# Attention with plain products on 64x32 and 64x64 tiles of the array, in front of an unchanged two-layer network

## The chip, the cores and the metric

The kernel runs on one core of a Trainium2 chip. The metric is the device time of one launch in microseconds (us). The core has a matrix engine (TensorE, called PE in the profile, with its weight loads as PEld), a vector engine (VectorE, DVE), an activation engine (ScalarE, ACT), a general engine (GpSimd, POOL), and queues that start DMA transfers (SP above all). Products are summed in PSUM, which has 8 banks of 128 partitions x 512 fp32 words; everything else lives in SBUF or in DRAM.

## The reference

Inputs are q, k, v of 8 batches x 8 heads x 576 positions x 64, and the network's weights (512 x 2048, 2048 x 512) and slopes.

```
scores = scale * np.matmul(q, k.transpose(0, 1, 3, 2))        # scale = 1/8
mask = block_i >= block_j                                      # blocks of 64 positions
scores = np.where(mask, scores, -1000000000.0)
scores = scores - np.max(scores, axis=-1, keepdims=True)
attn = np.exp(scores)
attn = attn / (np.sum(attn, axis=-1, keepdims=True) + 1e-09)
x = np.matmul(attn, v)            # then heads side by side: 4608 tokens x 512
h = x @ w_in
g = np.maximum(h, 0.0) + alpha * np.minimum(h, 0.0)
out = g @ w_out
```

A query block T (of nine, 0 to 8) sees the T + 1 key blocks 0 to T.

## The kernel before

**Two stages.** The 64 (batch, head) problems are taken as 32 pairs of heads, p = 0 to 31, four pairs to a batch. In the first stage attention of all pairs runs, and between its steps the network is computed for the first 6 of 16 feature groups (FA = 6) on chunks of 256 tokens (`chunk_a`: `ffn1` at L586, `activate` at L597 to L606, `ffn2` at L623, partial sums to DRAM). When attention has ended and the rest of these chunks too, the second stage takes the other 10 groups with chunks of 512 tokens (`factors`, `pair1` at L664, `ffn2` again) by a scheme of seven products in place of eight. There every operand is split into a high and a low part (hi, lo), each of which TensorE multiplies in one pass (type fp32r), and three products stand for one fp32 product.

**Attention per pair.** `prep` loads q, k and v, splits q and k into hi and lo (L745, L747, L750, L751), and lays them out by ten DMAs on the SP queue as stacked operands Q and K of 128 rows, in which hi and lo parts and the rows of a mask share one product. `query_tile` takes a tile j of 128 queries with all keys that any of them sees: products (L848, for the last 64 queries of both heads L921), a row maximum on DVE (L866, L872, L927), exp with row sums on ACT (L875, L934), the reciprocals on DVE, a scaling on POOL (L883, L941), transposes of 128x128 blocks on PE by a product with the identity (L891, L947, L956), and copies out of PSUM as hi (L970, ACT) and lo (L971, DVE). `values` multiplies with v: three products for one, again (L1004), and an ACT copy and a DVE sum that move the two parts together (L1023, L1025). For the first pairs (p below 5 in `values`, fewer in `query_tile`) plain fp32 products are used instead, which PE takes in two passes each: L853 (two heads on the two halves of the array's rows, 64x128 each), L856 (the mask), L915, L994 and L998.

**Weights.** `to_f32` (L468 to L485) makes fp32 words out of the 64-bit floats that are loaded, with five DVE instructions and one ACT instruction per 128x512 weights, and two PSUM banks for what lies between. `split` (L491, L492) makes hi on ACT and lo on POOL or DVE.

**Order.** Every instruction is handed to a planner (`Plan.op`, with an engine, a cost, the tiles it reads and writes and a priority), and `Plan.schedule` writes the order of every engine's queue and of every buffer's uses once, before the launch. `LAG` says by how many pairs the chunks run behind attention, `SHIFTS` changes single priorities, `BANKS`, `HB` and `AB` share the PSUM banks out: 6 for attention and weights, 1 for `ffn1`, 1 for `ffn2`.

Of the kernel before, what the change touches and what calls it, by code (L numbers as in the profile page):

```python
# [9 lines left out]
F32 = mybir.dt.float32  # L10
# [10 lines left out]
NP = H // 2  # L21
# [9 lines left out]
NEG = -1.0e30  # L31
SM = 512
QP = S + 64
PW = 1920
# [4 lines left out]
C0, C1 = 3.0, 4.0  # L39
WARM, WARM_END = 10, 3400  # L40
TICK, FULL_COLUMNS, SP0 = 3413.33, 3060, 700
LAG = 6.75
Q2B, TB = 1, 1
VP, VL, VE = 2.0, 1.0, 0.0
E0, E1 = -4.0, 1.0
NEAR, LP = 8.0, 1.0
FP = -1
XP = 2.0
AHEAD = {(8 + k // 2, k % 2): 12 + 4 * k for k in range(4)}
SHIFTS = {  # L50
# [6 lines left out]
}  # L57
SOON, XB = 150, 1006.7
FEW = 12
# [4 lines left out]
NV = NP + 1  # L64
PB = 6
# [8 lines left out]
IN_ORDER = {"qraw", "kraw", "vraw", "QH", "QL", "KH", "KL", "Q", "K", "V", "raw", "m", "xb", "X", "xt"}  # L74
# [16 lines left out]
class Plan:  # L91
# [44 lines left out]
    def schedule(self):  # L136
# [43 lines left out]
        while events:  # L180
# [13 lines left out]
            for engine, heap in ready.items():  # L194
# [12 lines left out]
                if engine == "PE" and before:  # L207

                    c, light = self.ops[chosen][1], None
                    if before.short and not c.light:  # L210
                        light = True
                    elif not before.short and c.light and not c.short:
                        light = False
                    if light is not None:
                        others = sorted(x for x in heap if (self.ops[x[1]][1].light if light else self.ops[x[1]][1].short)
                                        and x[0] < self.ops[chosen][5] + NEAR)
                        other = next((x for x in others if lacks(x[1]) is None), None)
                        if other:
                            heap.remove(other)
                            heap.append((self.ops[chosen][5], chosen))  # L220
                            heapq.heapify(heap)
                            chosen = other[1]
# [8 lines left out]
                if engine == "PE":  # L231
                    saved = before.short if before and cost.light else 0.0
# [52 lines left out]
HALF = 126  # L285
# [6 lines left out]
class Products:  # L292


    def __init__(self, full, rest, columns, short=0.0, light=False):
        self.full, self.rest, self.columns = full, rest, columns
        self.short, self.light = short, light

    def __add__(self, o):
        return Products(self.full + o.full, self.rest + o.rest, self.columns + o.columns) if o else self  # L300

    __radd__ = __add__
# [7 lines left out]
def c_mm(n, rows=P):  # L310
    return Products(max(n / 2.22, 107) + 2, max(n / 1.2, 213), n * rows / P)


def c_tr(light=False):
    return Products(109, 213, 256, 50.0, light)


def c_one(n, light=False):

    c = c_mm(n)  # L320
    return Products(c.full, c.rest, c.columns, c.full - max(n / 2.22 + 2, 57), light)
# [3 lines left out]
def attn_ffn(ctx, tc, qT, kT, vT, w_in, w_out, alpha, out):  # L325
# [14 lines left out]
    ident = const.tile([P, P], F32, name="ident")  # L340
    make_identity(nc, ident)
    mask_l = const.tile([P, P], BF16, name="mask_l")
    mask_r = const.tile([P, 64], BF16, name="mask_r")
    nc.vector.memset(mask_l, 0.0)
    nc.vector.memset(mask_r, 0.0)
    for i in range(2):
        nc.vector.memset(mask_l[64 * i:64 * i + 1, 0:64], 1.0)
        nc.vector.memset(mask_r[64 * i:64 * i + 1, :], NEG)
    oal = const.tile([P, NF], F32, name="oal")
    P4 = const.tile([P, 2, 64], F32R, name="P4")  # L350
# [17 lines left out]
    pt0 = ExitStack()  # L368
    pool0 = pt0.enter_context(tc.tile_pool(name="pt0", bufs=1, side="right"))
    PTF = [pool0.tile([P, 2, PW], F32, name=f"PTF{i}") for i in range(2)]  # L370
    KX = pool0.tile([P, 384], F32, name="KX")
    P4F = [pool0.tile([64, 2, 64], F32, name=f"P4F{i}") for i in range(2)]
    sp = att.enter_context(tc.tile_pool(name="sp", bufs=1))
    pt = []

    def pt_key(p):
        return p % 2 if p < NV else 2

    def pt_of(p, i):

        if i == 2:
            return P4F[p % 2] if p < NV else P4
# [791 lines left out]
```

## Time and profile before

| | |
|---|---|
| time, median of 3 runs (lowest, highest) | 1127.56 us (1124.86, 1128.02) |
| profiled execution, first to last instruction | 1122.8 us |
| median of the runs less that span | 4.8 us |
| busy: PE, PEld, DVE, ACT, POOL | 1105.6, 987.0, 833.1, 712.6, 610.3 us |
| last DVE sum of `values` (L1025) starts | 579.9 us |
| first product of the second stage (L664) | 642.8 us |

The profile has one execution. A row names a line of the kernel, an engine, an operation, the tiles written and read, and shapes as partitions x elements; for a matmul the shape with a star is that of the weights (rows*columns), and the next is the moving operand. "x60 | 18.3, 441" is 60 instructions, 18.3 us in which at least one ran, 441 ns from start to end of one. Matmuls overlap in that sense, since a new one starts while the former one's results drain, so their spacing is shorter than their length. An fp32 product stands as two MATMUL rows (two passes), one of type fp32r as one.

### The profile page before, as it was taken

The numbers are of one execution on the slowest core, as the hardware profiler recorded it, in microseconds if no ns is written. First come the engines' busy times: TensorE is split into PE (matmuls) and PEld (weight loads), VectorE is DVE, ScalarE is ACT, GpSimd is POOL, SyncE is SP. The second block draws the span as 40 slices with busy tenths as digits, with TensorE's granted clock in tenths as the row PEclk, the third lists the DMA queues.
The fourth block names the chain that finished last, engine by engine and source line by source line (L and its number), as shares of the span: only waits on it lengthen the run. The fifth ranks groups of instructions, "written<-read, shape, count | busy, mean of one in ns | idle before, by whom it ended". The sixth has DMA issues, their size and how long they took to land.

```text
span 1122.8 us, 22041 instructions
## 1 busy us (share of the span) xinstructions
PE 1105.6 (98%) x7288; PEld 987.0 (88%) x7288; DVE 833.1 (74%) x1962; ACT 712.6 (63%) x1933; POOL 610.3 (54%) x767
## 2 busy tenths in 40 slices
PE   7999999999999999999999999999999999999998
PEld 4667989999999999999998889988988988988987
DVE  6898888898888888898868898564647465656554
ACT  6889988888888788788856555343434334343432
POOL 4766557646555665466649897243434334352422
PEclk9999999999999999999999999999999999999999
DMA  7797677766665667567334332221303030312021
GB/s 220 232 266 216 184 229 184 197 181 184 196 169 145 180 175 215 165 175 205 100 112 148 115 121 84 76 75 39 113 1 113 1 113 4 111 38 76 1 76 38
DMA packets 75266, 147.96 MB, mean 132 GB/s; under 512 B 9744, under 2 KB 11792, under 8 KB 75152
## 3 DMA queue, kind: packets, MB, share of 16 engines
q1 hardware_dynamic: 74720, 146.28, 44.3%
q8 instruction: 58, 0.95, 0.4%
q14 instruction: 56, 0.46, 0.1%
q10 hardware_dynamic: 432, 0.27, 0.1%
HBM read 68.40 MB, written 29.36 MB: 87 GB/s over the span
## 4 chain that ended last, share of the span: by engine, by line
PE 87%; POOL 4%; DVE 4%; ACT 2%; issue 2%; DMA 1%; ACTq 0%; POOLq 0%; DVEq 0%
PE bank L623 33%; PE bank L664 19%; PE bank L586 11%; PE bank L1004 6%; PE bank L848 6%; PE bank L891 6%; PE bank L921 2%; PE bank L994 2%; PE bank L947 1%; POOL gl L606 1%; POOL w L492 1%; POOL xl L574 1%; DMA vraw<-in_v 1%; DVE QL L747 1%; ACT p L875 1%
## 5 line engine op out<-in xcount | busy, mean ns | idle before, releaser
L606 POOL TENSOR_TENSOR gl<-g,gh 128x256 fp32r<-128x256 f32 x288 | 221.3, 777 | 322.3 <-PE bank L664 162.1
L664 PEld LDWEIGHTS bank<-X,w 128*128 128x128 f32 x1890 | 253.3, 189 | 19.9 <-POOL X L492 0.9
L664 PE MATMUL bank<-X,w 128*128 128x256 f32 x1890 | 258.5, 281 | 0.5 <-POOL X L492 0.5
L623 PE MATMUL bank<-w,gh 128*128 128x512 f32 x720 | 225.7, 394 | 0.0
L597 ACT ACTIVATE g<-bank 128x256 f32<-128x256 f32 x288 | 110.3, 385 | 164.7 <-DVE bank L677 140.0
L883 POOL TENSOR_SCALAR p<-p,ri 128x256 f32<-128x256 f32 (+3 forms) x256 | 147.7, 589 | 101.0 <-DVE ri L881 57.2
L603 ACT CAST gh<-g 128x256 fp32r<-128x256 f32 x288 | 116.8, 407 | 79.7 <-DVE g L599 77.8
L599 DVE SCALAR_TENSOR_TENSOR g<-g,oal,bank 128x256 f32<-128x256 f32 x288 | 136.0, 476 | 38.1 <-ACT g L597 32.6
L677 DVE TENSOR_TENSOR bank<-bank,g 128x256 f32<-128x256 f32 x180 | 75.9, 428 | 103.4 <-PE bank L664 100.9
L875 ACT ACTIVATE p<-bank,nm 128x256 f32<-128x256 f32 (+3 forms) x256 | 134.3, 531 | 18.4 <-DVE nm L872 9.5
L623 PE MATMUL bank<-w,gl 128*128 128x512 f32 x360 | 141.9, 394 | 0.4 <-POOL gl L606 0.4
L623 PE MATMUL bank<-wa,gh 128*128 128x512 f32 x432 | 140.9, 407 | 0.2 <-POOL wa L492 0.2
L623 PEld LDWEIGHTS bank<-w,gh 128*128 128x128 f32 x720 | 120.7, 188 | 13.1
L586 PE MATMUL bank<-xh,wa 128*128 128x256 f32 x864 | 130.3, 287 | 1.9 <-DVE xh L572 1.7
L971 DVE TENSOR_TENSOR PL<-bank,PH 128x512 fp32r<-128x512 f32 (+2 forms) x189 | 111.6, 608 | 15.6 <-ACT PH L970 13.6
L586 PEld LDWEIGHTS bank<-xh,wa 128*128 128x128 f32 x864 | 115.8, 190 | 6.5 <-DVE xh L572 2.3
L891 PE MATMUL bank<-ident,p 128*128 128x128 f32 x640 | 109.2, 278 | 2.4 <-POOL p L883 1.6
L970 ACT CAST PH<-bank 128x512 fp32r<-128x512 f32 (+2 forms) x189 | 96.2, 529 | 10.8 <-PE bank L891 8.0
L848 PE MATMUL bank<-K,Q 128*128 128x512 f32 (+1 forms) x472 | 100.8, 329 | 0.1
L673 DVE TENSOR_TENSOR g<-bank,g 128x256 f32<-128x256 f32 x135 | 56.7, 422 | 48.4 <-PE bank L664 47.3
L891 PEld LDWEIGHTS bank<-ident,p 128*128 128x128 f32 x640 | 76.2, 142 | 16.4 <-POOL p L883 7.8
L872 DVE TENSOR_REDUCE nm<-bank 128x1 f32<-128x384 f32 (+3 forms) x144 | 81.5, 585 | 9.4 <-PE bank L848 6.5
(122 smaller groups left out, 2006.6 us busy)
## 6 DMA issues: line engine op xcount, KB each, us to landing
Q<-QH SPq DMA_DIRECT2D x62, 256.0 KB, 3.7
K<-KH SPq DMA_DIRECT2D x124, 128.0 KB, 3.6
vraw<-in_v SPq DMA_DIRECT2D x32, 320.0 KB, 3.3
qraw<-in_q SPq DMA_DIRECT2D x31, 320.0 KB, 3.4
xd<-xT SPq DMA_DIRECT2D x8, 1152.0 KB, 5.7
part<-o SPq DMA_DIRECT2D x36, 256.0 KB, 2.7
xb<-xd SPq DMA_DIRECT2D x9, 1024.0 KB, 5.4
m<-part SPq DMA_DIRECT2D x36, 256.0 KB, 3.4
```

The lines of the kernel that those rows point to most:

```text
L586: nc.tensor.matmul(hp()[:, :n], ww()[:, 0, cc * P:(cc + 1) * P], x()[:, cc, :n], start=(i == 0 and cc == 0), stop=(i == 2 and cc == NCC - 1))
L597: op("ACT", c_act(CHA), lambda: nc.scalar.activation(out=g(), in_=hp()[:, ts], func=AF.Relu, scale=-1.0), r=[hp], w=[g], prio=FP)
L599: op("DVE", c_dve(CHA) + 60, lambda: nc.vector.scalar_tensor_tensor(out=g(), in0=g(), scalar=oal[:, f:f + 1], in1=hp()[:, ts], op0=ALU.mul ...
L603: op("ACT", c_act(CHA, True), lambda: nc.scalar.copy(out=gh(), in_=g()), r=[g], w=[gh], prio=FP)
L606: op("POOL", c_pool(CHA), lambda: nc.gpsimd.tensor_tensor(out=gl(), in0=g(), in1=gh().bitcast(F32), op=ALU.subtract), r=[g, gh], w=[gl], p ...
L623: nc.tensor.matmul(acc(), a()[:, ts], ww(), start=(first and i == 0), stop=(last and i == 2))
L664: nc.tensor.matmul(bank()[:, :CHA], W()[:, i, 256 * at + P * c:256 * at + P * c + P], B()[:, j, CHA * c:CHA * c + CHA], start=(n == 0), st ...
L848: nc.tensor.matmul(o, Q()[:, i, qs], K()[:, 2 * h + i, :w], start=(i == 0), stop=(i == 1))
L875: op("ACT", 238 + w / 1.2, lambda h=h, t=t: nc.scalar.activation(out=t()[:, :w], in_=sb[h]()[:, off[h]:off[h] + w], func=AF.Exp, bias=nm() ...
L883: op("POOL", 244 + w / 1.2, lambda h=h: nc.gpsimd.tensor_scalar(out=pts[h]()[:, :w], in0=pts[h]()[:, :w], scalar1=ri()[:, h:h + 1], scalar ...
L891: nc.tensor.transpose(out=tp()[:, base + c * P:base + (c + 1) * P], in_=pts[h]()[:, c * P:(c + 1) * P], identity=ident)
L971: op("DVE", c_dve(n) + (HALF if n == P else 0), lambda: nc.vector.tensor_tensor(out=lo(), in0=src(), in1=hi().bitcast(F32), op=ALU.subtrac ...
```

## The change

**Attention's products are plain fp32.** No hi and lo parts of q, k, v or of the probabilities, no stacked operands, no mask rows. `scores` takes a list of query blocks T in one go, (8, 6), (7, 5) and (4, 3, 2, 1, 0) of a pair. The 64 queries of a block are cut into two lots of 32, and the keys of its T + 1 blocks into two sets, the first and the second 32 keys of each block. That gives four results of 32 partitions each (i = 0 to 3), which lie on the four groups of 32 PSUM partitions, and for the two heads (64 rows of the array each) on two PSUM banks, a "duo". So a block is eight products of weights 64x32 with 32 (T + 1) moving columns, one for each of the eight 64x32 tiles of the array. A query has its scores on two partition groups, half of its keys on each. Only keys that a query sees are multiplied, so nothing has to be masked.

**Softmax.** DVE takes the maximum of each partition, POOL exchanges it with the other partition group (`swap`, four instructions of 32 partitions), DVE takes the smaller of the two negated maxima, and ACT makes the exp with a sum for each partition. The 32x32 blocks are transposed by VectorE (`nc.vector.transpose`). The sums of both groups are brought together in `factors_of` (another `swap`, a DVE sum, four reciprocals, a transpose that spreads them), and used as factors after the product with v.

**Values.** `values` multiplies 64x64 weights (a key half block by the 64 values of a head; v is loaded twice, once for each half of the rows) with the transposed probabilities on the four 64x64 tiles. One DVE product with the factors writes the result to xT.

**Around it.** Three duos (six banks) serve scores and values. `to_f32` keeps its intermediates in one SBUF tile `ef` and has four DVE instructions, two on ACT and one on POOL. Half of the hi casts in `chunk_a` go to POOL (`GH`), some lo splits of later weights to DVE (`LATER`). `LAG` is 8.5, `SHIFTS` is empty, and the planner's rule on light and short products gives way to one on tiled products (`SWITCH`).

```diff
-HALVES = (((4, 3, 2), (2 * P, S, 1)), ((1, 0), (0, 2 * P, 0)))
-BANKS, HB, AB, HT, AM, AT, WB = 6, 1, 1, 3, 2, 4, 4
+TOP, MID, LOW = (8, 6), (7, 5), (4, 3, 2, 1, 0)
+FIRST, THEN = (3, 2, 1, 0), (4,)
+DUOS, HB, AB, HT, AM, AT, WB = 3, 1, 1, 3, 2, 4, 4
-LAG = 6.75
+LAG = 8.5
+SWAP = "POOL"
+PM, PX, PT, PZ, PU = -7, -5, 0.0, 0.0, 0
+GH, XH, XC = ("ACT", "POOL"), "DVE", 2
+LATER = ("DVE", "POOL", "DVE", "POOL", "DVE", "DVE")
...
+        op("ACT", c_act(512, True), lambda: nc.scalar.activation(out=ef()[:, 1], in_=fr(), func=AF.Copy, scale=2.0 ** -20), w=[(ef, 1)], prio=prio)
...
+        op("POOL", c_pool(512), lambda: nc.gpsimd.tensor_tensor(out=mb(), in0=mb(), in1=e().bitcast(F32), op=ALU.mult), r=[(ef, 0)], w=[mb], prio=prio)
...
+    def blocks(ap, n, j0):
+        return ap[:, :64 * n].rearrange("p (j x) -> p j x", x=64)[:, :, j0:j0 + 32]
+
+    def prep(p, pr):
+        q, k, v = Buf("q"), Buf("k"), Buf("v")
+        op("SP", 288, lambda: nc.sync.dma_start(out=q(), in_=qT[p]), w=[q], prio=pr)
+        op("SP", 288, lambda: nc.sync.dma_start(out=k(), in_=kT[p]), w=[k], prio=pr)
+        op("SP", 576, lambda: nc.sync.dma_start(out=v(), in_=vT[p]), w=[v], prio=pr + VL)
...
+    def swap(t, to, of, n, keys, key, scale, pr):
+        engine, cost = {"DVE": (nc.vector, 70), "POOL": (nc.gpsimd, 200)}[SWAP]
+        for i in range(4):
+            a, b = slice(32 * i, 32 * i + 32), slice(32 * (i ^ 1), 32 * (i ^ 1) + 32)
+            op(SWAP, cost, lambda a=a, b=b: engine.tensor_scalar(out=t()[a, to, n], in0=t()[b, of, n], scalar1=scale, scalar2=None, op0=ALU.mult),
+               r=keys, w=[(*key, i)], prio=pr)
...
+        def qk_run():
+            for T in Ts:
+                w = 32 * (T + 1)
+                for i in range(4):
+                    for h in range(2):
+                        hs, qs = slice(64 * h, 64 * h + 64), slice(64 * T + 32 * (i // 2), 64 * T + 32 * (i // 2) + 32)
+                        nc.tensor.matmul(sb()[32 * i:32 * i + 32, h, off[T]:off[T] + w], q()[hs, qs], blocks(k()[hs], T + 1, 32 * (i % 2)),
+                                         start=True, stop=True)
...
+            op("DVE", c_dve(2 * w), lambda t=t, w=w, o=o: nc.vector.tensor_reduce(
+                out=c()[:, 0, 2 * t:2 * t + 2], in_=sb()[:, :, o:o + w], axis=AX.X, op=ALU.max, negate=True), r=[sb], w=[(c, "n", t)], prio=pr + PM)
...
+            for h in range(2):
+                op("ACT", 388 + w / 1.2, lambda x=2 * t + h, T=T, h=h, w=w, o=o: nc.scalar.activation(
+                    out=pb()[:, 2 * o + h * w:2 * o + h * w + w], in_=sb()[:, h, o:o + w], func=AF.Exp, bias=c()[:, 2, x:x + 1], scale=0.125,
+                    accum_out=z()[:, 0, 2 * T + h:2 * T + h + 1]), r=[sb, (c, "m")], w=[(pb, t, h), (z, "s", T, h)], prio=pr + PX)
+            to, a = pts[T > 3], at_T(T)
+            op("DVE", 186 + 2 * w, lambda to=to, a=a, w=w, o=o: nc.vector.transpose(out=to()[:, a:a + 2 * w], in_=pb()[:, 2 * o:2 * o + 2 * w]),
+               r=[(pb, t, 0), (pb, t, 1)], w=[(to, T)], prio=pr + PT)
...
+        def run():
+            for i, (a, e) in zip(parts, ranges):
+                for j in range(e):
+                    T = max(j, a)
+                    for h in range(2):
+                        start, step, m = run_of(T, e, h, j)
+                        for g in range(2):
+                            gs = slice(64 * g, 64 * g + 64)
+                            x = pts[i]()[gs]
+                            x = bass.AP(x.tensor, x.offset + 32 * start, [x.ap[0], [32 * step, m], [1, 32]])
+                            nc.tensor.matmul(ob()[64 * h:64 * h + 64, g, 32 * T:32 * e], v()[gs, j, h, :], x, start=(j == 0), stop=(j == e - 1))
...
+        op("DVE", c_dve(64 * (T1 - T0)), lambda: nc.vector.tensor_tensor(
+            out=xT[:, pair, r0 + 64 * T0:r0 + 64 * T1].rearrange("p (t g x) -> p g t x", g=2, x=32), in0=view(ob), in1=view(R), op=ALU.mult),
+            r=[ob, R], w=[("x", b % 2, pair, i) for i in parts], prio=pr + PU)
```

More of the change, by code (lines that the diff above doesn't have):

```diff
@@ L71 @@
 TO_POOL = 70
-IN_ORDER = {"qraw", "kraw", "vraw", "QH", "QL", "KH", "KL", "Q", "K", "V", "raw", "m", "xb", "X", "xt"}
+IN_ORDER = {"q", "k", "v", "p", "PTL", "PTH", "z", "r", "R", "raw", "m", "ef", "xb", "X", "xt"}
 class Buf:
@@ L206, in schedule @@
                     continue
[L207 to L222, printed above, removed]
+                if engine == "PE" and before and before.tiled and not self.ops[chosen][1].tiled:
+                    others = sorted(x for x in heap if self.ops[x[1]][1].tiled and x[0] < self.ops[chosen][5] + NEAR)
+                    other = next((x for x in others if lacks(x[1]) is None), None)
+                    if other:
+                        heap.remove(other)
+                        heap.append((self.ops[chosen][5], chosen))
+                        heapq.heapify(heap)
+                        chosen = other[1]
                 _, cost, _, _, bufs, _, then = self.ops[chosen]
@@ L231, in schedule @@
                 if engine == "PE":
-                    saved = before.short if before and cost.light else 0.0
+                    saved = SWITCH if before and before.tiled and cost.tiled else 0.0
                     before = cost
@@ L292, with __init__ @@
 class Products:
[L295 to L302, printed above, removed]
+    def __init__(self, full, rest, columns, tiled=False):
+        self.full, self.rest, self.columns, self.tiled = full, rest, columns, tiled
     def __mul__(self, k):
@@ L532, in later_weights @@
             W = w1s[f] = Buf("w1")
-            ms = [later(f + i, 0, *((prio(f), ["att"], "words") if f > FA else (SOON, [], "att"))) for i in range(2)]
+            ms = [later(f + i, 0, *((prio(f), ["att"]) if f > FA else (SOON, []))) for i in range(2)]
             (m0, w0), (m1, w1) = ms
@@ L974, in values @@
-    def values(p, v_parts, spans, pr):
-        V, vkeys = v_parts
+        parts = []
+        for p0, p1 in ((0, 1), (1, NP)):
+            for i, (src, queue) in enumerate(((qT, "SP"), (kT, "ACTQ" if p0 == 0 else "SP"))):
+                issuer = {"SP": nc.sync, "ACTQ": nc.scalar}[queue]
+                cs = slice(S + 256 * i, S + 256 * i + 256)
+                op(queue, 128 * (p1 - p0), lambda p0=p0, p1=p1, src=src, issuer=issuer, cs=cs: issuer.dma_start(
+                    out=xT[:, p0:p1, cs], in_=src[p0:p1, :, :256].rearrange("p r n -> r p n")), w=[("qk"[i], p) for p in range(p0, p1)], prio=pr + i)
@@ new lines, in early_loads, with early, at_T, run_of @@
+        for p in range(NP):
+            parts.append((lambda p=p: xT[:, p, S:S + 256], lambda p=p: xT[:, p, S + 256:S + 512],
+                          [("q", p), ("k", p), ("x", 1, p, 0), ("x", 1, p, 1)]))
+        return parts
+    def early(p, pr):
+        v = Buf("v")
+        op("SP", 256, lambda: nc.sync.dma_start(out=v()[:, :4], in_=vT[p, :, :4]), w=[v], prio=pr)
+        return v
+    def at_T(T):
+        u = T - 4 if T > 3 else T
+        return 32 * u * (18 if T > 3 else 8)
+    def run_of(T, T1, h, j):
+        u, step = (T - 4, 18 + h) if T > 3 else (T, 8 + h)
+        start = step * u + h * (5 if T > 3 else 1) + j
+        return start, step, T1 - T
@@ L1029, in xs @@
     def xs(b, parts=(0, 1)):
[L1030 removed]
+        return [("x", b % 2, pr, i) for pr in range(NP) for i in parts]
     def spill(b, pr):
@@ L1084, in more_room @@
               ("m", 2, [512], F32), ("ws", 1, [512], F32), ("xt", 2, [512], F32), ("g", 4, [CHA], F32))
+        for i in range(2 * DUOS):
+            plan.room("bank", 1, lambda slot, i=i: plan.tiles["duo"][i // 2][:, i % 2])
         plan.quota["hp"] += HT - HB
         plan.quota["acc"] += AM - AB
-        plan.quota["words"] = WB
     op("NONE", 0, end_attention, r=xs(B - 1), w=["att"], prio=0, then=more_room)
```

513 lines of the change are left out of this document (109 added, 404 removed), and 6 rows, old and new, of the table SHIFTS.

## The prediction

> **What bounds the kernel now.** First the page: its busy line, three lines of its slices, and the chain that ended last.
>
> ```profile
> PE 1105.6 (98%) x7288; PEld 987.0 (88%) x7288; DVE 833.1 (74%) x1962; ACT 712.6 (63%) x1933; POOL 610.3 (54%) x767
> ...
> PE   7999999999999999999999999999999999999998
> ...
> DVE  6898888898888888898868898564647465656554
> ...
> PE 87%; POOL 4%; DVE 4%; ACT 2%; issue 2%; DMA 1%; ACTq 0%; POOLq 0%; DVEq 0%
> ```
>
> PE is full from the second slice on and makes up 87% of the chain. So a product that goes is worth its time on PE, as long as nothing else fills the place. DVE is the next engine: eight to nine tenths in the first twenty slices, where attention runs. The busy time by stretches, for all engines and then for the two PE lines of the network's first part, and the first product of the second stage:
>
> ```profile
> 0.00:100.00 100.00, 90.59 (x513) 62.73 (x514) 81.14 (x216) 79.70 (x216) 63.02 (x88) 0.98 0.83 242
> 100.00:580.00 480.00, 478.65 (x3434) 443.99 (x3433) 411.23 (x1053) 402.27 (x1157) 280.79 (x385) 1.00 0.63 173
> 580.00:650.00 70.00, 67.68 (x423) 59.98 (x422) 56.32 (x92) 40.28 (x91) 64.02 (x65) 1.00 0.49 164
> ...
> 0.00:580.00 580.00, 157.36 (x1057) 139.67 (x1058) 1.00 0.66 185
> 0.00:580.00 580.00, 146.69 (x513) 88.02 (x513) 1.00 0.66 185
> ...
> L664 PE MATMUL bank<-X,w x1890: 274/281/390, 642.8 to 1110.5; 128*128 128x256 f32 x189
> ```
>
> Columns after the stretch's length: PE, PEld, DVE, ACT, POOL, then the granted clock and the DMA share. Until 580 us PE works 569.2 of 580 us. It starts 1057 products of 256 columns (L586) and 513 of 512 columns (L623) there. Their busy times overlap other lines, so I price them by the chain in the second stage, which repeats exactly:
>
> ```profile
> 763.00 2.78 PE bank L623 x12
> ...
> 773.53 2.79 PE bank L623 x12
> ```
>
> Twelve take 2.78 us, 0.232 us each. The period is 10.53 us and holds 24 of them and 42 products of 256 columns (L664), which leaves (10.53 - 5.56) / 42 = 0.118 us for one of these. So the network takes 1057 x 0.118 + 513 x 0.232 = 244 us of the 569, the ten warm-up products 2, and **attention 323 us**. That is what the change replaces; the 480 us from 642.8 on keep their products.
>
> **The new products.** How fast plain fp32 passes run, alone and on two tiles of rows, stands in the timeline of the start:
>
> ```profile
> 13.76 0.86 PE L994 MATMUL bank<-PTF,vraw 128*64 128x256 f32 x4
> 16.71 1.51 PE L994 MATMUL bank<-PTF,vraw 128*64 128x256 f32 x8 [0.15 <-ACT PTF L968]
> 18.15 0.70 PE L853 MATMUL bank<-KX,xT 64*128 64x256 f32 x4
> 21.08 0.49 PE L853 MATMUL bank<-KX,xT 64*128 64x128 f32 x4
> ...
> 14.56 0.30 PEld L853 LDWEIGHTS bank<-o,xT 64*128 64x128 f32 x4 [0.17 <-issue]
> 16.36 0.20 PE L856 MATMUL bank<-mask_r,mask_l 64*128 64x64 bf16 x2
> ...
> 108.85 0.19 PE L1004 MATMUL bank<-P,V 128*128 128x64 f32 x1
> 108.88 0.48 PE L1004 MATMUL bank<-PL,V 128*64 128x320 f32 x2
> ```
>
> Four L994 passes are two of 256 and two of 128 columns, 768 in all, and eight are 1536: (1.51 - 0.86) / 768 = 0.85 ns per column and pass. The L853 passes, two heads on two row tiles, gain 0.21 us for 512 columns more: 0.41 ns. Half: the two tiles run side by side, both passes of each. That is shown for two tiles of rows. Tiles of columns side by side are not in this trace.
>
> Scores: the nine blocks have 32 x (1 + ... + 9) = 1440 moving columns, each for eight tiles and two passes. If all eight overlap, that is 2 x 1440 x 0.85 = 2.44 us a pair; if only the two row tiles do, four times that, 9.8. Values: the nine key blocks have 10 x 32 + 35 x 32 = 1440 columns too, on four tiles: 2.44 us or 4.9. I take 4.9 us for the sum, since the row nearest to it shows independent tiles, and keep 14.6 as the other end.
>
> Each of four tiled runs a pair interrupts 128-row products. At the way in, the L853 loads stand 0.17 us with nothing to wait for, then their own first load shows. I take 0.3 us for way in and out together, bounds 0.1 and 0.5: 1.2 us a pair. Sum 6.1 us; 32 pairs, and 8 more runs since the first four pairs are done in two goes (2 us), make **197 us in place of 323: 126 us less**. With the bounds of the switch 171 to 223.
>
> **The other engines, which must keep up.** The rows nearest to the new instructions:
>
> ```profile
> L866 DVE TENSOR_REDUCE nm<-bank 128x2 f32<-128x512 f32 x28 | 19.1, 682 | 2.7 <-PE bank L848 2.6
> L866 DVE TENSOR_REDUCE nm<-bank 128x2 f32<-128x256 f32 x28 | 11.6, 415 | 0.8 <-PE bank L848 0.7
> L881 DVE RECIPROCAL ri<-sp 128x2 f32<-128x2 f32 x128 | 20.5, 160 | 5.6 <-POOL gl L606 0.4
> L599 DVE SCALAR_TENSOR_TENSOR g<-g,oal,bank 128x256 f32<-128x256 f32 x288 | 136.0, 476 | 38.1 <-ACT g L597 32.6
> L572 DVE CAST xh<-xT 128x512 fp32r<-128x512 f32 x24 | 15.1, 654 | 0.3 <-PE bank L586 0.2
> L482 DVE SCALAR_TENSOR_TENSOR m<-raw,bank 128x512 f32<-128x512 uint32 x32 | 21.5, 677 | 0.1
> ...
> 15.65 0.75 DVE L872 TENSOR_REDUCE nm<-bank 128x1 f32<-128x256 f32 x2
> ...
> 16.55 0.48 ACT L875 ACTIVATE p<-bank,nm 128x256 f32<-128x256 f32 x1
> 17.02 0.47 ACT L875 ACTIVATE p<-bank,nm 128x256 f32<-128x256 f32 x1
> ...
> L875 ACT ACTIVATE p<-bank,nm 128x512 f32<-128x512 f32 x64 | 44.1, 691 | 3.4 <-DVE nm L872 2.0 <-DVE ri L940 1.0
> L875 ACT ACTIVATE p<-bank,nm 128x128 f32<-128x128 f32 x64 | 23.2, 368 | 6.7 <-DVE nm L866 1.8 <-DVE nm L872 1.7 <-DVE ri L881 1.5
> L473 ACT ACTIVATE bank<-m,ebias 128x512 int32<-128x512 int32 x32 | 22.2, 695 | 4.0 <-DVE m L470 3.7
> ...
> L751 POOL TENSOR_TENSOR KL<-kraw,KH 128x576 fp32r<-128x576 f32 x31 | 46.8, 1509 | 13.8 <-ACT KH L750 11.8 <-DVE nm L930 1.3 <-POOL p L883 0.6
> L492 POOL TENSOR_TENSOR w<-m,w 128x512 fp32r<-128x512 f32 x20 | 27.8, 1392 | 2.5 <-ACT w L491 2.5
> L883 POOL TENSOR_SCALAR p<-p,ri 128x128 f32<-128x128 f32 x64 | 26.5, 424 | 12.6 <-DVE ri L881 7.7 <-ACT pl L934 1.7 <-ACT QH L745 1.2
> ```
>
> DVE, per pair: nine maxima over 2880 elements at 1.04 ns and 148 ns each by L866, 4.3 us. Nine transposes of the same sizes: no row has one; I take a maximum's price again, 4.3, below it half (a DVE that moves two elements a step), above it twice. The transpose of the factors and the last product, 576 elements each, 1.5; eight small ones at 0.16, 1.3. That is 11.5 us of records. Two of 0.415 us end within 0.75 (L872), so a follower starts 0.08 us before the record ahead of it ends: 9.2 us of pace. Before, DVE was busy 492 us until 580; less 88 L599 (42), casts (15 in the row, some 24 with the narrower ones) and 18 weights of five instructions (61), 365 us or 11.4 a pair. So DVE gets **no lighter**. What else it has to do by the end of attention is 80 L599 (32), casts (20), 18 weights of four instructions (43): 295 + 95 = 390 us at pace, some 480 in records.
>
> ACT, per pair: 18 exps. One of 256 with its sum starts 0.47 us after the one before, which over 2880 elements at 0.83 ns (0.691 us of record at 512 columns less 0.368 at 128, over 384) gives 0.25 a piece and 2.4: 7 us, against 402 + 80 = 482 us of ACT for all until 580. About 90 us of copies and casts for the network stay, so 310 in place of 482. POOL: 16 swaps a pair; L883 at 128 columns takes 0.424 us, so up to 0.4 each, 6.4 us; KL (1.5 us) and eight scalings of 0.42 and more go, 4.9 at least. ACT gets lighter, POOL hardly, DVE not.
>
> DMA: ten copies a pair for Q and K leave the SP queue, v grows from 320 to 576 KB; the share was 0.63 and PE the bound, so nothing from that.
>
> Waits that are new: the exps of a group stand behind a swap on POOL, in whose queue gl (L606) and the lo parts lie. Behind a late exp stand the transposes, and the duo stays taken. The first stage has a reserve against that: 62 us of the network's products came after attention (580 to 643), with LAG 8.5 in place of 6.75 more is meant to be left, and PE can take them up while a group waits. Weights after attention: 14 go through the one `ef`, each a chain of four DVE instructions, two of ACT and one of POOL, some 5.4 us by these rows (2.7, 1.3 and 1.4), 75 in a line. POOL was busy 64 of 70 us there.
>
> **The sum**, against the profiled 1122.8 us, 4.8 us under the median of 1127.56: 1122.8 - 126 = 997. PE idles 10.8 us until 580 and 2.3 until 650 now. I add 28 us more: 10 at the start, where less PE work meets the same chain of DVE, ACT and POOL; 8 for groups that wait for DVE; 10 at the change of stage. That makes 1025, and with 4.8 **1030 us**; with the switch at its bounds and idle of 10 to 50, 985 to 1078.
>
> **Rivals.**
>
> *Column tiles take turns (the other side).* If only the row tiles overlap, as far as the trace shows, attention needs (14.6 + 1.2) x 32 + 2 = 508 us of PE: 1122.8 + 185 + 28 + 4.8 = 1340. It turns slower from a product time of 8 us a pair on (8.0 + 1.2 = 9.2; 32 x 9.2 + 2 + 28 = 323), 1.6 times the ideal. For it: nothing overlaps by columns here. Against it: both passes of two row tiles ran together, so tiles keep their own place in the queue. Chance 0.06.
>
> *A floor under each pass.* A pair has (72 + 52) x 2 = 248 passes, and 4.9 us give 20 ns to each. The two L856 passes end within 0.20 us although one alone takes 0.19, so two start within 10 ns; yet the closest two full-array products of L1004 start 30 ns apart (27 of them streaming). At 30 ns: 7.4 + 1.2 = 8.6 us, 279 in all, 1112 us. Chance 0.07. The Trainium skill, TensorEngine Tiling (Array Packing), section Instruction Overhead, speaks for such a floor: some 60 cycles for each matmul, so that a dimension that is small already should not be cut. As an estimate from that page, 25 ns a pass, the sum would be some 1072 us. The pair of L856 rows speaks against it, for two in a row only.
>
> *DVE, or the chain through swap and duo, paces attention.* With DVE at its records' 480 us and filled as from 100 to 580 now (411 of 480, 0.86) attention ends near 560 and the remaining network takes at least 40: 600 in place of 643, so 1080 + 4.8 = 1085. For it: DVE 0.86 full with the same load per pair, while a pair's share of the time shrinks from 18 us (580 / 32) to 14 (460 / 32, if 85 of 545 are left for later). Against it: in pace DVE needs 390. Chance 0.18.
>
> *All of it comes through.* Switch 0.1 us and no more idle than now: 1122.8 - 323 + 171 + 4.8 = 976. Chance 0.10.
>
> *The gain is eaten exactly*, by DVE and the start together: about 1125. Chance 0.02.
>
> **How the numbers follow.** The forecast has 0.57, its own range 995 to 1060. 985 to 1090 takes in the pace of DVE and half of the best case, and leaves the floor and the column tiles out. 0.3% (3.4 us) is about what can be told from no change. Faster is the forecast, the best case, nearly all of the DVE case (0.17) and of the floor 0.04: 0.88. Same 0.03; slower 0.09, from the column tiles and a floor over 34 ns.
>
> **What would show it.** Right: PE near 0.95 of the first stage, the tiled lines together near 200 us of spacing, eight tiles' rows starting within some 50 ns, the first L664 near 545 us. Wrong on tiles: rows of a group of eight start one after the other. Wrong on the floor: low blocks as long as high ones. Wrong on DVE: PE waits for transposes or for a duo, and DVE over nine tenths. Wrong on the change of stage: PE idle before the first L664, released by POOL or DVE.

## The result and the profile after

The changed kernel takes 1117.19 us (1116.18 to 1117.36, four runs), the kernel before 1126.21 us on the same chip (1124.61 to 1128.02): a ratio of 0.9918 with a 95% interval of 0.9904 to 0.9932. So it is faster by 9 us or 0.8%, little but outside the noise; the forecast was 1030 us (range 985 to 1090), 96 us less than this 1126.21. The sections below look for the other 87 us.

The page of the changed kernel, its own time 1114.4 us: the busy line, three lines of its slices (the last is TensorE's granted clock), and the engines' shares of the chain that ended last.

```profile
PE 1034.5 (93%) x12860; PEld 873.4 (78%) x12860; DVE 788.8 (71%) x1830; ACT 550.1 (49%) x1926; POOL 576.6 (52%) x1048
...
PE   5657899999999999999988989999999999999998
...
DVE  6898898888888878884766975656555555555553
...
PEclk9676899999999999999999999999999999999999
...
PE 71%; DVE 13%; POOL 8%; issue 4%; ACT 4%; DMA 0%; ACTq 0%; DVEq 0%; POOLq 0%
```

PE's own work fell by 71 us (1105.6 to 1034.5), but its share of the chain fell from 87 to 71%, and DVE's rose from 4 to 13: the chain now runs through waits that were not there. In the first four slices, 0 to 111 us, PE is five to seven tenths busy. The same stretches of the two kernels, cut where the start is over, where the attention ends and where the second stage's first product stands (columns as in the prediction). Before:

```profile
0.00:120.00 120.00, 110.52 (x654) 81.05 (x655) 99.03 (x262) 99.01 (x272) 75.18 (x103) 0.99 0.81 234
120.00:580.00 460.00, 458.72 (x3293) 425.67 (x3292) 393.34 (x1008) 382.95 (x1102) 268.63 (x369) 1.00 0.62 172
580.00:643.00 63.00, 61.13 (x378) 54.24 (x377) 49.42 (x77) 34.50 (x79) 58.21 (x60) 1.00 0.46 157
643.00:1122.00 479.00, 475.23 (x2970) 426.05 (x2968) 291.26 (x619) 196.14 (x483) 208.26 (x235) 1.00 0.19 64
```

After:

```profile
0.00:120.00 120.00, 75.92 (x1477) 54.68 (x1481) 98.37 (x248) 67.89 (x261) 80.20 (x168) 0.76 0.48 160
120.00:510.00 390.00, 387.40 (x7937) 321.34 (x7927) 331.69 (x877) 243.06 (x1089) 216.36 (x572) 1.00 0.37 122
510.00:603.00 93.00, 82.35 (x488) 70.49 (x487) 60.87 (x89) 41.15 (x88) 72.62 (x79) 1.00 0.35 118
603.00:1114.00 511.00, 488.82 (x2973) 426.90 (x2971) 297.89 (x619) 197.99 (x488) 207.41 (x230) 1.00 0.18 59
```

Three things stand here. Up to 120 us PE is busy 75.9 us in place of 110.5, and at 0.76 of the clock in place of 0.99. From 120 us to the end of attention it is full (387.4 of 390), as forecast. And the second stage, whose products are the same (x2973 and x2970), takes 511 us in place of 479, with 22 us of PE idle in place of 4. The other 14 us stand in PE's busy time (488.8 for 475.2): a record of such a product lasts some 280 ns while the next one starts after 118, so each wait also lays bare the end of the product before it.

The new tiles themselves do what was hoped. One run of scores in the timeline of the changed kernel, 112 passes, with the first full product after it:

```profile
300.34 1.97 PE L712 MATMUL duo<-k,q 64*32 64x256 f32 x112
302.24 0.50 PE L496 MATMUL bank<-xh,wa 128*128 128x256 f32 x2
```

1.90 us for 112 passes is 17 ns each. A floor of 25 or 30 ns under each, or column tiles that take turns (four times the time), would have made it 2.8, 3.4 or over 6 us.

### The profile page after: what moved, and what is told of

It is laid out like the page before. It is cut to its first block, busy times and chain, and to the rows that moved or that the text cites. A ratio compares the mean times of both kernels' runs of the same rounds, so it can differ in the third digit from the quotient of the medians.

```text
span 1114.4 us, 32213 instructions
## 1 busy us (share of the span) xinstructions
PE 1034.5 (93%) x12860; PEld 873.4 (78%) x12860; DVE 788.8 (71%) x1830; ACT 550.1 (49%) x1926; POOL 576.6 (52%) x1048
## 4 chain that ended last, share of the span: by engine, by line
PE 71%; DVE 13%; POOL 8%; issue 4%; ACT 4%; DMA 0%; ACTq 0%; DVEq 0%; POOLq 0%
PE bank L535 15%; PE duo L535 13%; PE duo L576 13%; PE bank L496 11%; PE duo L767 7%; PE duo L712 7%; PE bank L576 3%; PE duo L496 3%; DVE g L509 3%; POOL c L692 2%; ACT g L507 2%; POOL gl L518 1%; DVE c L717 1%; DVE duo L589 1%; DVE g L585 1%
## 5 line engine op out<-in xcount | busy, mean ns | idle before, releaser
L725 ACT ACTIVATE p<-duo,c 128x160 f32<-128x160 f32 (+8 forms) x576 | 219.8, 402 | 53.2 <-DVE c L720 48.0
L576 PEld LDWEIGHTS duo<-X,w 128*128 128x128 f32 x1470 | 198.3, 189 | 32.0 <-DVE g L509 9.3
L576 PE MATMUL duo<-X,w 128*128 128x256 f32 x1470 | 209.3, 284 | 10.4 <-DVE g L509 6.2
L535 PE MATMUL duo<-w,gh 128*128 128x512 f32 x520 | 165.5, 399 | 7.3 <-DVE g L509 5.9
L692 POOL TENSOR_SCALAR c<-c 32x4 f32<-32x4 f32 (+3 forms) x400 | 99.1, 248 | 91.4 <-DVE c L717 65.1
L717 DVE TENSOR_REDUCE c<-duo 128x2 f32<-128x320 f32 (+8 forms) x288 | 125.6, 482 | 16.8 <-PE duo L712 14.8
L515 ACT CAST gh<-g 128x256 fp32r<-128x256 f32 x234 | 94.8, 406 | 78.9 <-DVE g L509 77.3
L725 ACT ACTIVATION_READ_ACCUMULATOR p<-duo,c 128x1 f32 x576 | 122.7, 213 | 0.0
L712 PE MATMUL duo<-k,q 64*32 64x288 f32 (+8 forms) x4352 | 107.3, 323 | 11.6 <-ACT p L725 6.3
L535 PE MATMUL duo<-w,gl 128*128 128x512 f32 x260 | 102.5, 394 | 0.3 <-POOL gl L518 0.2
L729 DVE STREAM_TRANSPOSE PTH<-p 128x576 f32<-128x576 f32 (+4 forms) x160 | 97.5, 625 | 0.8 <-ACT p L725 0.5
```

Source lines behind the costliest of these rows:

```text
L515: op("ACT", c_act(CHA, True), lambda: nc.scalar.copy(out=gh(), in_=g()), r=[g], w=[gh], prio=FP)
L535: nc.tensor.matmul(acc(), a()[:, ts], ww(), start=(first and i == 0), stop=(last and i == 2))
L576: nc.tensor.matmul(bank()[:, :CHA], W()[:, i, 256 * at + P * c:256 * at + P * c + P], B()[:, j, CHA * c:CHA * c + CHA], start=(n == 0), st ...
L692: op(SWAP, cost, lambda a=a, b=b: engine.tensor_scalar(out=t()[a, to, n], in0=t()[b, of, n], scalar1=scale, scalar2=None, op0=ALU.mult), r ...
L712: nc.tensor.matmul(sb()[32 * i:32 * i + 32, h, off[T]:off[T] + w], q()[hs, qs], blocks(k()[hs], T + 1, 32 * (i % 2)), start=True, stop=True)
L717: op("DVE", c_dve(2 * w), lambda t=t, w=w, o=o: nc.vector.tensor_reduce(out=c()[:, 0, 2 * t:2 * t + 2], in_=sb()[:, :, o:o + w], axis=AX.X ...
```

## The second stage: waits that are not there in the data

PE's three longest waits in the second stage, changed kernel (engine, tile and line, waited for; us in total, times, longest):

```profile
PE duo L576 <- DVE g L509: 6.2, 8, 1.6
PE duo L535 <- DVE g L509: 5.9, 9, 1.5
PE duo L576 <- DVE g L585: 2.2, 3, 1.1
...
```

The same view of the kernel before:

```profile
PE bank L664 <- POOL X L492: 0.5, 2, 0.3
PE bank L623 <- POOL gl L606: 0.4, 1, 0.4
```

All but 1.1 us of the waits in the changed kernel's view are on `duo`. Once attention is over, the change takes six of the eight banks as the two halves of three two-bank tiles; 1470 of the 1890 products of L576 go to such a half. The timeline of the changed kernel at a place where both kernels run the same products:

```profile
830.46 0.39 PE L535 MATMUL duo<-w,gl 128*128 128x512 f32 x1
830.60 0.47 DVE L509 SCALAR_TENSOR_TENSOR g<-g,oal,duo 128x256 f32<-128x256 f32 x1
...
831.13 0.74 PE L576 MATMUL duo<-X,w 128*128 128x256 f32 x4 [0.28 <-DVE g L509]
```

and of the kernel before:

```profile
799.79 0.40 PE L623 MATMUL bank<-w,gl 128*128 128x512 f32 x1
799.94 0.47 DVE L599 SCALAR_TENSOR_TENSOR g<-g,oal,bank 128x256 f32<-128x256 f32 x1
800.02 0.89 PE L664 MATMUL bank<-X,w 128*128 128x256 f32 x6
```

Before, the product starts while DVE still reads another bank. After, it starts when DVE's instruction has ended (830.60 + 0.47), since the bank that DVE reads is the other half of the tile that it writes. The theory: the framework orders accesses by tile, and one half waits for the other half's reader. The rival: the hand-set shifts of the order are gone and some of the subtractions for the later weights went to DVE (four of six for each two feature groups, by the instruction counts), so the order itself got worse. Two kernels tell them apart; neither changes the order of instructions on any engine.

**Six banks of their own** (`e1_banks`), in the changed kernel:

```diff
+    psd = att.enter_context(tc.tile_pool(name="psd", bufs=1, space=PSUM))
-    rooms(ps, ("duo", DUOS, [2, 512], F32), ("bank", 8 - 2 * DUOS, [512], F32))
+    rooms(psd, ("duo", DUOS, [2, 512], F32))
+    rooms(ps, ("bank", 8 - 2 * DUOS, [512], F32))
...
+        pools["ps2"] = ctx.enter_context(tc.tile_pool(name="ps2", bufs=1, space=PSUM))
-        for i in range(2 * DUOS):
-            plan.room("bank", 1, lambda slot, i=i: plan.tiles["duo"][i // 2][:, i % 2])
+        rooms("ps2", ("bank", 2 * DUOS, [512], F32))
```

> Edit: the three two-bank duos of the attention come from a PSUM pool of their own, which is closed with the attention; six tiles of one bank each replace the six halves after it. The order of the instructions on each engine stays that of the changed kernel. Theory (false waits: a product on one half waits for VectorE or ScalarE work on the other half, because both halves are one tile): the second stage goes back from 511 us to 480 (475 to 488) and a part of the 8 us that PE waits between 510 and 603 us goes too, so the time is about 1083 us (1075 to 1092). Rival (the stage grew because its order has lost the hand-set shifts, or because two of its subtractions moved to VectorE): the order is the same, so the stage stays at 508 to 514 us and the time at 1114 to 1120.

Measured: 1087.73 us, ratio to the kernel before 0.9652 (0.9634 to 0.967). PE's waits in its second stage:

```profile
PE bank L578 <- POOL w L402: 3.3, 1, 3.3
PE bank L578 <- POOL X L402: 2.0, 1, 2.0
PE bank L578 <- DVE g L511: 0.6, 2, 0.4
```

The waits on halves are gone, and 29.5 us with them. The time lies in the theory's range, the stage does not: its length is 491 us (594.9 to 1086.2), not 480: the chunks of 512 tokens after the first start 52.8 to 53.2 us apart, nearly as before (52.6 to 52.8), but the first one, in which the last weights are still being converted, 59.0 in place of 49.0 (from the first to the 211th product of L578). That is the change of stage, for which 10 us were forecast. The first stage gained 8.5 us (603.4 to 594.9); its last part had used halves too.

**The kernel before with halves** (`e4_halves`):

```diff
-    rooms(ps, ("bank", 8, [512], F32))
+    rooms(ps, ("duo", 3, [2, 512], F32))
+    for i in range(6):
+        plan.room("bank", 1, lambda slot, i=i: whole(i // 2)[:, i % 2])
+    rooms(ps, ("bank", 2, [512], F32))
```

> Edit: the kernel before, its order of instructions kept; six of its eight PSUM banks are taken as halves of three two-bank tiles. Theory (false waits): the second stage grows from 480 us by the same 25 to 35 us, the attention's stage too, since its products then also wait on the other half, by 5 to 30 us: 1155 to 1195 us. Rival (halves cost nothing, the loss is of order): 1124 to 1130 us.

Measured: 1295.88 us, 1.15 times the kernel before (1.1476 to 1.1523). The price in the attention was far above what was expected (its second stage starts at 790.5 us in place of 642.8), in the second stage a little under it (503 us in place of 480, where 25 to 35 more were expected). Its first two waits there are of the kind seen above:

```profile
PE duo L632 <- DVE g L608: 4.2, 8, 1.0
PE duo L632 <- ACT g L606: 1.8, 2, 1.1
...
```

So the theory is shown in both directions, with the order held fixed: false waits between halves cost the change 29.5 us.

## The start: what holds PE up to 120 us

PE's longest waits up to 120 us in the changed kernel:

```profile
PE duo L712 <- ACT p L725: 8.2, 4, 3.3
PE bank L496 <- ACT wa L399: 6.3, 4, 3.9
PE duo L712 <- DVE xT L773: 4.9, 3, 2.8
PE bank L535 <- POOL gl L518: 3.9, 2, 3.5
PE bank L535 <- ACT gh L515: 3.4, 2, 2.0
PE bank L535 <- POOL wa L400: 3.2, 2, 2.3
...
```

No single source: scores wait for a duo that an exp still reads, the network for weights. The lo parts of the first twelve weights come at 41.9 to 118.6 us (18.3 to 97.3 before). Until they are there the network's products cannot fill PE, and a pair's attention now gives PE 6.5 us where it gave 10, while DVE needs as long as ever (366 us of records for the 32 pairs, 11.5 each, as the prediction had it). The chain that ended last names GpSimd most from 20 to 120 us: its swaps of the maxima (L692) have 16.8% of that stretch, its parts of the weights' conversion (L394, L400) 7.4% each, while the largest share of a DVE line, the maxima (L717), is 4.0%.

Candidates: the conversions (one after the other through the single `ef`), the chain of maximum, swap, minimum and exp, the swaps' place in GpSimd's queue, or simply DVE's load. In all the runs of this section the planner lays the order of the instructions anew, which by the last two of them moves the time by 5 to 11 us of itself; smaller differences decide nothing here.

**Two buffers for the conversion** (`e2_ef2`, on the changed kernel):

```diff
-    rooms(wraw, ("raw", RB, [1024], I32), ("m", EB, [512], F32), ("ef", 1, [2, 512], F32))
+    rooms(wraw, ("raw", RB, [1024], I32), ("m", EB, [512], F32), ("ef", 2, [2, 512], F32))
```

> Edit: two buffers in place of one for the exponents and fractions of a weight's conversion, so that two conversions can be under way. Theory A (the start is held by conversions that come one after the other through the one buffer, 7 us each): the last of the first twelve weights is ready 15 to 30 us earlier than 118.6 us, PE is busy over 70 us of the first 100 (63.3 before), and the time falls by 8 to 20 us. Theory B (VectorE, busy some 18 of each 20 us from 20 to 100 us, sets the pace of the start): the weights come at most 5 us earlier, PE's share stays within 3 us, time within 4 us of 1117.

Measured: 1121.77 us (1121.5 to 1122.4), ratio to before 0.9953, 4.6 us slower than the changed kernel; PE busy 60.9 of the first 100 us, and the last weight ready at 117.0 us. Not the buffer: theory A falls.

**No conversions at the start** (`e3_noconv`, on the changed kernel):

```diff
-                mb, w = to_f32(src[f].bitcast(I32), prio, early=E0 - 6.5 if f + i == 0 else None)
+                mb = w = Buf("m")
+                op("SP", 256, lambda w=w, i=i, f=f: nc.sync.dma_start(out=w(), in_=qT[2 * f + i, :, :512]),
+                   w=[w], prio=E0 - 6.5 if f + i == 0 else prio)
```

> Edit: the first twelve weights are not converted from 64-bit words; 128x512 values of another input are loaded in their place, so six loads of a kind, the AND, OR and sum on VectorE, two ScalarE passes and the GpSimd product of each are left out (the outputs are then those of other weights). Theory A (the conversions cost the start): PE busy over 85 us of the first 100, the first product of the second stage some 25 to 35 us before 603.1, 1080 to 1092 us in all. Theory C (the attention's own chain of maximum, swap, exponent, transpose holds the start, not the conversions): PE busy under 72 us of the first 100, the second stage at most 10 us earlier, 1107 to 1117 us.

Measured once: 1095.75 us, 21 us less; PE busy 75.5 of the first 100 us; both lie between the two theories. So the conversions cost about 21 us (a single run, which `e9_both` bears out), and something else holds the start as well. The other runs stand on the kernel with six banks of its own, 1087.7 us, so that the waits of the second stage don't blur them.

**No maxima** (`e5_nomax`):

```diff
-            op("DVE", c_dve(2 * w), lambda t=t, w=w, o=o: nc.vector.tensor_reduce(
-                out=c()[:, 0, 2 * t:2 * t + 2], in_=sb()[:, :, o:o + w], axis=AX.X, op=ALU.max, negate=True), r=[sb], w=[(c, "n", t)], prio=pr + PM)
-        keys = swap(c, 1, 0, slice(0, n), [(c, "n", t) for t in range(len(Ts))], (c, "o"), 0.125, pr + PM)
-        op("DVE", 75, lambda: nc.vector.scalar_tensor_tensor(out=c()[:, 2, :n], ...
...
-                    ... func=AF.Exp, bias=c()[:, 2, x:x + 1], scale=0.125,
+                    ... func=AF.Exp, bias=zero, scale=0.125,
```

> Edit, on the kernel with six banks of their own (1087.7 us): the maxima of the scores, their swaps on GpSimd and the smaller of the two are left out, the exponent is taken of the unshifted scores. Theory (VectorE and GpSimd hold the first 120 us, in which PE waits 47 us between the products of that kernel): 20 us of VectorE's and 22 us of GpSimd's work of 20 to 120 us go, so PE's idle time up to 120 us falls to under 32 us, and the time by 12 to 25 us to 1063 to 1076. Rival (only the arrival of the weights counts, since from 120 us on PE is busy 99%): the last of the twelve weights is no earlier than 5 us, 1081 to 1089 us.

Measured: 1056.41 us, ratio to before 0.938 (0.9361 to 0.94): 31.3 us less than with the maxima, more than expected. The second stage starts at 565.3 us.

**Swaps on VectorE** (`e6_swap`):

```diff
-SWAP = "POOL"
+SWAP = "DVE"
```

> Edit, on the kernel with six banks of their own: the swaps of the two partition groups, four small instructions each, go from GpSimd to VectorE. Theory 1 (the start and the attention are at VectorE's pace, 94 of the 100 us from 20 to 120 us): 16 more instructions of some 0.2 us a pair make VectorE slower than PE, the attention ends 30 us or more later than 511 us, 1110 us or above. Theory 2 (the start is held by the swaps' turn in GpSimd's queue behind its products of 1.3 us): the start gets shorter, PE idle under 40 us up to 120 us, 1075 to 1088 us.

Measured: 1154.01 us, ratio 1.0243 (1.0225 to 1.0262). The 94 of 100 us in the expectation were a sum of rows, whose records overlap; the window shows 87. Here DVE is busy 109 of the first 120 us and 366 of the next 380, and PE idles from beginning to end of the attention: theory 1.

**No maxima and no conversions** (`e9_both`: the edits of `e5_nomax` and `e3_noconv` together):

> Edit, on the kernel without maxima (1056.4 us): the first twelve weights are not converted either; 128x512 values of another input are loaded in their place (the outputs are then those of other weights). Theory (the start is VectorE's and GpSimd's work, whatever it is for: what the conversions cost comes on top of what the maxima cost): PE idle under 18 us up to 120 us (29.6 with the conversions), the second stage's first product at 545 to 556 us (565.3), 1036 to 1048 us. Rival (one of the two is enough to free the start; what is left is the filling of the pipeline): 1051 to 1058 us.

Measured: 1033.88 us, ratio 0.9179 (0.9154 to 0.9204): another 22.5 us, a little more than the theory's range, and the two prices add up. The second stage starts at 541.9 us.

**The conversion of the kernel before** (`e10_conv`, shortened: the first twelve weights get the old five DVE instructions, with a duo's halves as scratch, and no product on GpSimd):

```diff
-        raw, ef, mb = Buf("raw"), Buf("ef"), Buf("m")
+        raw, ef, mb = Buf("raw"), None if at_first else Buf("ef"), Buf("m")
+        if at_first:
+            dd = Buf("duo")
+            eb, fb = ((lambda j=j: dd()[:, j]) for j in range(2))
...
+            op("DVE", c_dve(512), lambda: nc.vector.scalar_tensor_tensor(
+                out=mb(), in0=mb(), scalar=2.0 ** -20, in1=eb(), op0=ALU.mult, op1=ALU.mult), r=[(dd, 0)], w=[mb], prio=prio)
+            return mb, mb
```

> Edit, on the kernel with six banks of their own (1087.7 us): the conversions of the first twelve weights are done as in the kernel before, with their scratch in the halves of a PSUM duo and their last product on VectorE (five VectorE instructions of some 0.68 us in place of four of 0.6 to 1.0 and one of GpSimd of 1.3). Theory A (the change's move of the conversion to SBUF and GpSimd holds the start: GpSimd makes 40% of the chain of 20 to 120 us): the last weight is ready over 10 us earlier, 1072 to 1082 us. Theory B (VectorE's pace: it gets 0.4 us more work for each weight, and the attention loses one of three duos meanwhile): 1090 to 1110 us.

Measured: 1089.25 us (1088.71 to 1089.69), ratio 0.9669, the same as with the new conversion within 1.5 us. Neither theory's range was met. The first 120 us of these kernels, by the windows view; first six banks of their own, then no maxima, swaps on VectorE, neither maxima nor conversions, and the old conversion:

```profile
0.00:120.00 120.00, 73.34 (x1442) 52.35 (x1445) 96.70 (x242) 66.72 (x254) 79.61 (x165) 0.72 0.48 160
```

```profile
0.00:120.00 120.00, 90.30 (x2205) 68.64 (x2209) 94.78 (x223) 86.06 (x353) 61.29 (x93) 0.87 0.59 193
```

```profile
0.00:120.00 120.00, 70.26 (x1285) 49.76 (x1293) 109.09 (x327) 59.90 (x227) 33.88 (x34) 0.73 0.44 146
```

```profile
0.00:120.00 120.00, 104.81 (x2671) 83.05 (x2672) 75.48 (x208) 85.97 (x398) 50.53 (x97) 0.96 0.60 196
```

```profile
0.00:120.00 120.00, 73.41 (x1564) 53.11 (x1564) 102.95 (x270) 63.75 (x259) 58.24 (x163) 0.80 0.50 163
```

Read the DVE and POOL columns against PE's. Where work of the maxima and the conversions goes, PE gets further (73 to 90 to 105 us busy), and the lo part of the last of the twelve weights comes earlier (at 120.7, 101.1 and 73.4 us). Without maxima DVE is as busy as before (94.8) and has done more pairs in that time. With the swaps moved to DVE, POOL does 46 us less and DVE 12 more, and everything is slower (last weight at 135.9 us). With the old conversion POOL does 21 us less and DVE 6 more, and PE gets no further (116.8 us). So the start is held by the work of the maxima and the conversions, which is shown by leaving it out, and not by GpSimd's queue alone, though that makes the largest part of the chain. That DVE's pace is the limit is the reading that fits all five rows, but it is argued: the two runs without work lighten GpSimd too, the other two load DVE while they lighten GpSimd, `e10_conv` takes a duo from attention as well, and none of them lightens DVE alone. In the kernel before, DVE was as full there (99.0), but PE had long products to go on with (110.5 us busy).

**Another order** (`e7_plan` and `e8_costs`). The expectation of `e7_plan` rests on a comparison with the planner's own plan, which no trace shows. `e8_costs` sets the planner's costs to the durations in the trace of the kernel with its own banks; `e7_plan` has these, moves the copies of x to ScalarE and one of six subtractions for the later weights to GpSimd, and gets new priorities (shortened):

```diff
-GH, XH, XC = ("ACT", "POOL"), "DVE", 2
+GH, XH, XC = ("ACT", "POOL"), "ACT", 2
...
-C0, C1 = 1, 3.5
+C0, C1 = -2, 3.25
...
-        op("DVE", c_dve(512), lambda: nc.vector.scalar_tensor_tensor(
+        op("DVE", 833, lambda: nc.vector.scalar_tensor_tensor(
```

> Edit, on the kernel with six banks of their own: the planner's costs of VectorE's, ScalarE's and GpSimd's instructions are set to the durations of that kernel's trace (907 ns in place of 598 for an instruction of 128x512 with both operands in SBUF, 0.33 in place of 0.08 us for the small sums), the copies of x for the first stage go from VectorE to ScalarE, and the priorities of the conversions and the attention are chosen anew by the planner with these costs. Theory (the order was laid out for a VectorE that is faster than it is; it fell 13 us behind the plan between 45 and 120 us and 10 more around the change of stage): 1065 to 1080 us. Rival (PE's own work and the waits for data that no order moves): 1084 to 1092 us.

> Edit, on the kernel with six banks of their own: the planner's costs alone are set to the durations of the trace, its other constants stay. Theory (the order is at fault): half of the gain of the run with the new priorities, 1074 to 1084 us. Rival: 1085 to 1095 us, the constants having been chosen for the old costs.

Measured: 1082.35 us (ratio 0.9607, 0.9586 to 0.9627) and 1098.57 us (0.975, 0.9735 to 0.9764). The first gains 5 us, less than the theory and a little more than its rival; the second loses 11, more than its rival allowed. Its first 120 us are no worse (PE 77.8 us), but PE idles 13.5 us from 600 to 700. So the order moves the time by 5 to 11 us, and neither of these two brings the 87 us back. `e7_plan` is the fastest kernel here that computes everything the reference does, ahead of both kernels.

## Why the prediction was wrong in size

The direction was right, and 1030 us was not: 87 us are missing. Three edits together take away 83: 29.5 (halves), 31.3 (the maxima's work) and 22.5 (the conversions' work at the start), from 1117.2 to 1033.9 us. The second and third are prices of work left out, not of faults in the change, so that the end lies 4 us from the forecast is no confirmation of it. They show what this work costs at the start, and the forecast had reckoned that PE would hardly see it. In the sum's own terms the 87 us are 29.5 for the halves, some 41 at the start above the 10, and 12 for the tiles, less some 6 of the 8 for waits on DVE: 77, as an estimate. About 10 are not accounted for.

**The step that failed first: "the 480 us from 642.8 on keep their products".** They do, and still take 511 us. The claim went from the same products to the same time and did not ask where their banks come from. The line that says so, `plan.tiles["duo"][i // 2][:, i % 2]`, was in the diff. It costs nothing on any engine; it was to be seen only by asking which instructions share a tile.

**The step that failed most: "10 at the start, where less PE work meets the same chain".** The mechanism was named and the size was off by five. PE is idle 44.1 of the first 120 us (9.5 before), and what it does runs at a lower clock. 110.52 us at 0.99 are 109 us of full-speed work, 75.92 at 0.76 are 58: a loss of 51 us by this estimate, near the 53.8 that the two removals give together. Some 35 of the 51 are idle time, and some 17 the lower clock (75.92 x 0.24, less 1 before), which the sum had no term for. The rows for it were there: DVE 81 of the first 100 us, "no lighter" by the prediction's own count, and PE's 10 us a pair shrunk to 6. As long as the twelve weights are not ready, PE can do no more than attention's chain through DVE and GpSimd feeds it, so what PE saved in that stretch turned into idle time. The forecast spread DVE's load over the whole attention, where there is slack, and not over the stretch where the filler is missing.

**What held.** The attention's price: from 200 to 500 us PE is busy 298.15 us, with 732 products of 256 and 354 of 512 columns and 4954 tiled passes, 248 to a full pair.

```profile
200.00:500.00 300.00, 298.15 (x6040) 249.00 (x6031) 255.97 (x674) 187.34 (x826) 170.34 (x439) 1.00 0.37 125
...
200.00:500.00 300.00, 102.63 (x732) 93.48 (x732) 1.00 0.37 125
200.00:500.00 300.00, 96.10 (x354) 61.74 (x355) 1.00 0.37 125
```

(298.15 - 732 x 0.118 - 354 x 0.232) / (4954 / 248) = 6.5 us a pair, against 6.1: 12 us in 32 pairs. (That PE's busy time fell by only 71 us, and not by 126, is no contradiction: the busy time of the changed kernel also holds the lower clock of the start and the ends laid bare by waits. The same 12860 rows take 1001.8 us in `e9_both`, 104 less than before.) "8 for groups that wait for DVE" was too much: from 120 to 510 us PE is idle 2.6 us. "10 at the change of stage" was right, once the halves are out of the way. DVE's transposes cost what a maximum of the same size does (760 and 751 ns on the mean at 576 columns), as assumed. ACT got lighter (712.6 to 550.1 us), POOL hardly (610.3 to 576.6).

**The rivals.** Column tiles in turn and a floor of 25 or 30 ns under each pass are refuted by the run of 1.90 us. The rule of the Trainium skill, TensorEngine Tiling (Array Packing), section Instruction Overhead, of some 60 cycles for each matmul does not hold for these tiles. Passes here start 17 ns apart on the mean, where the prediction's estimate from that page was 25. That the floor of 30 ns gave 1112 us, 5 from the measured time, is luck. "The gain is eaten exactly, by DVE and the start together", about 1125 us at a chance of 0.02, came next and named the start; but a third of the missing 87 us are the halves, which stood in no case, so part of that is luck as well. "DVE paces attention" (1085) was wrong in place: attention ended at 510 us and not near 560, and it paced only the first 120 us. The forecast's own end of attention, 460 us (85 of 545 left for later), was missed by 50 us, about the loss at the start. The range was too narrow at the top because it had this rival and the forecast apart: the start of the one and the body of the other both came true.

## What to carry to other kernels

When a change takes work from the engine that is full, look for the stretch in which the next engine was already as full and count there, not over the stage: here, what was saved turned into idle time until other work could fill it. When buffers are regrouped, ask for each instruction which tile it touches: views of one tile are ordered against each other even where they share no byte, and each bank that is used by itself wants a tile of its own. A kernel whose order stays fixed while the tiles change shows such waits in one run.

## What the runs showed of the hardware

**VectorE against GpSimd.** The change moved a conversion's scratch from PSUM to SBUF. Its instructions then vary, where they had not. Three groups of the changed kernel by line (min, median and max in ns), all on DVE:

```profile
L387 DVE SCALAR_TENSOR_TENSOR ef<-raw,ef x32: 643/712/1587, 26.8 to 648.0; 128x512 int32<-128x512 int32 x32
...
L384 DVE TENSOR_SCALAR ef<-raw x32: 381/426/1516, 13.3 to 647.6; 128x512 int32<-128x512 int32 x32
...
L737 DVE SCALAR_TENSOR_TENSOR z<-z x36: 135/176/1277, 15.7 to 507.6; 128x18 f32<-128x18 f32 x28, 128x8 f32<-128x8 f32 x4, 128x10 f32<-128x10 f32 x4
```

and one of the kernel before, where one operand was in PSUM:

```profile
L482 DVE SCALAR_TENSOR_TENSOR m<-raw,bank x32: 666/678/689, 13.5 to 683.3; 128x512 f32<-128x512 uint32 x32
```

The timeline of the changed kernel shows the longest of the small sums:

```profile
71.94 1.28 POOL L394 TENSOR_TENSOR m<-m,ef 128x512 f32<-128x512 f32 x1
71.97 1.28 DVE L737 SCALAR_TENSOR_TENSOR z<-z 128x10 f32<-128x10 f32 x1
...
73.17 0.77 DVE L729 STREAM_TRANSPOSE PTH<-p 128x576 f32<-128x576 f32 x1
```

Ten columns take as long as the GpSimd product beside them, and the transpose comes behind. The Trainium skill, SBUF — State Buffer, section SBUF: two separate sides, says that the two engines share a pair of ports under an exclusive lock, held for a whole instruction, for which a DVE instruction with two SBUF inputs competes. The traces agree: 1.28 us where the median is 0.18, and hardly any spread with one operand in PSUM (666 to 689 ns). L384 has a single SBUF input and varies too (381 to 1516 ns), which that sentence does not cover. What this costs the kernel was not separated: with PSUM scratch for the first weights (`e10_conv`) it is no faster, but has one more DVE instruction for each of them.

**The clock.** In the changed kernel the granted clock is 0.76 over the first 120 us, in which PE is busy 63% of the time, and 1.00 behind; with PE busy 87% there (neither maxima nor conversions) it is 0.96. A 512-column product takes 0.80 us at 90.58 us, in that start, and 0.39 at 299.78. So where PE had to wait in these runs, it also worked more slowly in between. The share of busy time does not settle the clock by itself: PE is busy 73 us of the first 120 both with six banks of its own and with the old conversion, at 0.72 and at 0.80.
